# Attention masks as bfloat16 products, maxima of four heads at once, and a second batch's sums moved

## The chip, the cores and the metric

The kernel runs on one core of a Trainium2 chip. The metric is the device time of one execution in microseconds (us). A core has five engines, each of which works through its own list of instructions in order and waits for the others by semaphores: TensorE (PE, with its weight loads PEld), VectorE (DVE), ScalarE (ACT), GpSimd (POOL) and SyncE (SP), which here issues all the DMAs.

## The reference

Two batches of 8 heads, 768 positions, head dimension 64, all in float32. Each query sees the keys less than 16 positions away and, beside them, 24 block summaries of its batch: per block of 32 positions the maximum of the keys and the mean of the values. The result goes through two feed-forward networks (512 to 2048 to 512), one after the other.

```python
k_sum = k.reshape(B, H, nb, 32, D).max(axis=3)
v_sum = v.reshape(B, H, nb, 32, D).mean(axis=3)
scores_l = np.where(abs(pos[:, None] - pos[None, :]) < 16, scale * q @ k.T, -1e9)
scores_s = scale * np.einsum('bhsd,bhnd->bhsn', q, k_sum) + np.log(32)
a = softmax(np.concatenate([scores_l, scores_s], axis=-1))
x = np.matmul(a, np.concatenate([v, v_sum], axis=2))
g = h - np.tanh(h)                # first network,  h = x @ w_in;  x = g @ w_out
g = h * np.tanh(softplus(h))      # second network, the same way
```

## The kernel before

The attention works in 12 units of 128 queries (units 0 to 5 are batch 0, units 6 to 11 batch 1). A unit has two row halves of 64 queries (`s`) and two head parities (`e`); with four pairs of heads (`hp`) that gives, for each `e`, a PSUM bank of 4 x 120 scores: 24 summaries and 96 window keys. The banks of `e` = 0 have the tag `s`, those of `e` = 1 the tag `tr`, two buffers each; `v_trans` takes a `tr` bank as well.

Everything is issued by one hand-written loop over steps j = 0 to 31. Each engine gets its instructions in that order. For unit u:

- step 2u: `qk(u)`, the products of queries and keys on TensorE (line 310). It needs `k_fill(u)`, which copies the block maxima into both ends of the unit's key tile (line 263).
- steps 2u+1 and 2u+2: `softmax(u, 0)` and `softmax(u, 1)`. On VectorE one instruction for each pair of heads adds the mask and reduces to the negated maximum (line 324); on ScalarE one exponential for each follows, with its sum (line 329).
- step 2u+3: `norm(u)`, reciprocals on VectorE (lines 336, 339), then one product for each `e` (line 341), on GpSimd, or on VectorE where `NORM_DVE` says so.
- steps 2u+5 and 2u+6: `a_trans(u, e)`, four transposes on TensorE (line 349) and a copy out of PSUM (lines 353 on VectorE, 355 on ScalarE, by `ASB_DVE`).
- step 2u+7: `av(u)`, the products with the values (line 363); steps 2u+8 and 2u+9: `x_hi` and `x_lo` split the result in two parts (lines 371, 375).

Within a step the order is `x_hi`, `qk`, `softmax`, weight conversions (`AHEAD`), `norm`, `x_lo`, `a_trans`, `av`, then a list `todo` filled by `at(step, ...)`: loads, `k_sum` (block maxima, line 255), `k_fill`, `v_sum` (block sums, line 272 on VectorE or lines 276 and 280 on GpSimd), and last more conversions (`AFTER`). A conversion (`conv_tick`) splits a piece of the weights, over ScalarE (`conv_top`, line 114; `conv_hi`), VectorE (`conv_or`, line 121; `conv_lo`, line 137) and, in the steps of `HI_POOL` and `LO_POOL`, GpSimd.

At steps 24, 25 and 29 the loop issues the first products of the first network (`more_in`), whose first 512 tokens are units 0 to 3. After the loop come 96 network steps.

Of the kernel before, what the change touches and what calls it, by code (L numbers as in the profile page):

```python
# [2 lines left out]

# [6 lines left out]
F32 = mybir.dt.float32  # L10
# [16 lines left out]
def kernel(  # L27
# [32 lines left out]
    BIG = 1.0e30  # L60
# [5 lines left out]
    n_raw, n_cv = 6, 5  # L66
# [11 lines left out]
    def pst(tag):  # L78
        return ps.tile([128, 512], F32, tag=tag, name=tag)
# [88 lines left out]

    ASB_DVE = (0, 2, 7, 11, 12, 13, 14, 15, 17, 20, 21)
    NORM_DVE = (0, 13, 21, 23)
    FILL_DVE = (0, 1, 4, 5, 6, 7, 8, 9, 11)
    AHEAD = {23: 1, 24: 3, 29: 3, 31: 1}
    AFTER = {19: 1, 21: 1, 22: 1, 25: 1, 28: 3, 30: 1}
    HI_POOL = (19, 21, 22, 24, 25, 30)
# [2 lines left out]
    def attention(actx):  # L179
        con = actx.enter_context(tc.tile_pool(name="con", bufs=1, side="right"))  # L180
        two = actx.enter_context(tc.tile_pool(name="two", bufs=2, side="right"))
# [3 lines left out]
        NK = UPB + 2  # L185
        kt = [kq.tile([128, HP, KU + 2 * NB], F32, name=f"kt{n}") for n in range(NK)]
        qt = [kq.tile([128, HP, 128], F32, name=f"qt{n}") for n in range(3)]
        vu = [con.tile([KA, 2, H, D], F32, name=f"vu{n}") for n in range(3)]
        masks = [con.tile([128, KA], F32, name=f"mask{m}") for m in range(3)]
        ident = con.tile([128, 128], F32, name="ident")  # L190
        SUM = ((0, NB), (KW, KA))
        WND = ((NB, KA), (0, KW))

        def constants():
            nonlocal tops
            make_identity(nc, ident)
            k_edges(0)
            for m in range(3):
                nc.gpsimd.memset(masks[m], 0.0)
                for s in range(2):  # L200
                    rows = masks[m][T * s:T * s + T]
                    nc.gpsimd.memset(rows[:, SUM[s][0]:SUM[s][1]], math.sqrt(D) * math.log(BLK))
                    reg = rows[:, WND[s][0]:WND[s][1]]

                    conds = [([[1, KW]], -1, -1), ([[-1, KW]], 2 * WIN - 1, 1)]
                    if (m, s) == (0, 0):
                        conds.append(([[1, KW]], -WIN, 0))
                    if (m, s) == (2, 1):
                        conds.append(([[-1, KW]], KW - WIN - 1, 0))
                    for pattern, base, mul in conds:  # L210
                        nc.gpsimd.affine_select(
                            out=reg, in_=reg, pattern=pattern, base=base, channel_multiplier=mul,
                            compare_op=ALU.is_ge, fill=-BIG,
                        )
            k_edges(UPB)
            tops = top_tiles(2)

        vtc, ksum, vsum = {}, {}, {}
# [39 lines left out]
            )  # L258

        def k_fill(u):  # L260
            eng = nc.vector if u in FILL_DVE else nc.gpsimd
            for o in (0, NB + KU):
                eng.tensor_copy(kt[u % NK][:, :, o:o + NB], ksum[u // UPB])

        def v_sum(b, g, part, pool=False):
            if b not in vsum:
# [31 lines left out]
        sums, neg, aa, asb, xps, sc = {}, {}, {}, {}, {}, {}  # L298

        def qk(u):  # L300


            for e in range(2):
                sc[u, e] = pst(("s", "tr")[e])[:, 0:HP * KA].rearrange("p (a n) -> p a n", a=HP)
            for hp in range(HP):
                for s in range(2):
                    for e in range(2):
                        d = slice(64 * e, 64 * e + 64)
                        k0 = s * (NB + T)
                        nc.tensor.matmul(  # L310
                            out=sc[u, e][T * s:T * s + T, hp, :],
                            lhsT=qt[u % 3][d, hp, T * s:T * s + T],
                            rhs=kt[u % NK][d, hp, k0:k0 + KA],
                        )

        def softmax(u, e):
            w, pv = u % UPB, sc.pop((u, e))
            if e == 0:
                aa[u] = two.tile([128, 2, HP, KA], F32, tag="aa", name="aa", bufs=3)
                neg[u] = two.tile([128, 2, HP], F32, tag="neg", name="neg", bufs=3)  # L320
                sums[u] = two.tile([128, 2, HP], F32, tag="sums", name="sums", bufs=3)
            m = masks[0 if w == 0 else 2 if w == UPB - 1 else 1]
            for hp in range(HP):
                nc.vector.tensor_tensor_reduce(  # L324
                    out=aa[u][:, e, hp, :], in0=pv[:, hp, :], in1=m, scale=-1.0 / math.sqrt(D),
                    scalar=3.0e38, op0=ALU.add, op1=ALU.min, accum_out=neg[u][:, e, hp:hp + 1],
                )
            for hp in range(HP):
                nc.scalar.activation(  # L329
                    out=aa[u][:, e, hp, :], in_=aa[u][:, e, hp, :], func=ACTF.Exp,  # L330
                    scale=-1.0, bias=neg[u][:, e, hp:hp + 1], accum_out=sums[u][:, e, hp:hp + 1],
                )

        def norm(u):
            r = two.tile([128, 2, 2, HP], F32, tag="rd", name="rd")
            nc.vector.tensor_scalar(
                out=r[:, 0], in0=sums[u], scalar1=1.0e-9, scalar2=None, op0=ALU.add
            )
            nc.vector.reciprocal(out=r[:, 1], in_=r[:, 0])
            for e in range(2):  # L340
                (nc.vector if 2 * u + e in NORM_DVE else nc.gpsimd).tensor_tensor(
                    out=aa[u][:, e], in0=aa[u][:, e],
                    in1=r[:, 1, e, :].unsqueeze(2).to_broadcast([128, HP, KA]), op=ALU.mult,
                )

        def a_trans(u, e):
            p = pst("aT")
            for hp in range(HP):
                nc.tensor.transpose(p[0:KA, hp * 128:(hp + 1) * 128], aa[u][:, e, hp, :], ident)
            t = two.tile([KA, HP, 128], F32, tag=f"asb{e}", name="asb")  # L350
            pv = p[0:KA, :].rearrange("p (a n) -> p a n", a=HP)
            if 2 * u + e in ASB_DVE:
                nc.vector.tensor_copy(t, pv)
            else:
                nc.scalar.activation(out=t, in_=pv, func=ACTF.Copy)
            asb[u, e] = t
# [26 lines left out]
        def at(u, *fs):  # L383
            todo.setdefault(u, []).extend(fs)
# [28 lines left out]
        at(4, L(load_k, 8), L(v_sum, 0, 1, 0), L(v_sum, 0, 2, 0), L(v_sum, 0, 2, 1, True))  # L413
        before_av[5] = L(v_trans, 0)
        at(5, L(v_fill, 1), L(v_fill, 2), L(load_k, 9), L(load_k, 10))
        at(5, L(k_sum, 6))
        at(6, L(k_sum, 7))
        at(7, L(k_sum, 8), L(load_k, 11))
        at(8, L(k_sum, 9), L(load_vt, 1, 0))
        at(9, L(k_sum, 10), L(load_vt, 1, 1))  # L420
        at(10, L(k_sum, 11), L(k_fill, 6))
        at(11, L(load_vt, 1, 2), L(v_sum, 1, 0, 0))
        at(12, L(v_sum, 1, 0, 1, True), L(conv_ahead, n_raw))
        at(13, L(v_sum, 1, 1, 0))
        at(14, L(v_sum, 1, 1, 1, True))
        at(15, L(v_sum, 1, 2, 0, True))
        at(16, L(v_sum, 1, 2, 1))
        before_av[17] = L(v_trans, 1)
        at(17, L(v_fill, 1), L(v_fill, 2))
        for u in range(7, 12):  # L430
            at(2 * u - 3, L(k_fill, u))
        NJ = 2 * NU
        LT, LA = 5, 6

# [4 lines left out]
        for j in range(NJ + LA + 2):  # L439
            if j in (NJ, NJ + 1, NJ + 5):  # L440
                more_in(n_in)
            if j == NJ:
                kq_x.close()
                more_w(4)
            xu, xr = divmod(j - LA - 2, 2)
            if xu >= 0 and not xr:
                x_hi(xu)
            if j < NJ and j % 2 == 0:
                qk(j // 2)
            nu, nr = divmod(j - 3, 2)  # L450
            nr = nr == 0 and 0 <= nu < NU
            if 1 <= j <= NJ:
                softmax(*divmod(j - 1, 2))
            ticks(j, AHEAD)
            if nr:
                norm(nu)
            if xu >= 0 and xr:
                x_lo(xu)
            if LT <= j < NJ + LT:
                a_trans(*divmod(j - LT, 2))  # L460
            if j in before_av:
                before_av[j]()
# [295 lines left out]
```

## Time and profile before

| | us |
|---|---|
| median of 3 runs (range) | 602.61 (602.38 to 603.33) |
| profiled execution: its time | 603.07 |
| its span, first to last instruction | 601.3 |
| busy in the span: PE, DVE, ACT, POOL | 578.8, 417.8, 328.5, 53.4 |

The span is 1.77 us shorter than the execution's time. In the slices of the page, of 15 us each, TensorE is at nine tenths or more from the ninth on; POOL works in the first six and hardly after. Matmul times overlap one another, so a busy TensorE in the attention isn't an engine at its limit.

### The profile page before, as it was taken

How to read it: one execution, taken by the hardware profiler on the slowest of the kernel's cores; microseconds unless marked ns; L12 is line 12 of the kernel's file. 1: busy time of each engine (PE TensorE's matmuls, PEld its weight loads, DVE VectorE, ACT ScalarE, POOL GpSimd, SP SyncE). 2: the span in 40 equal slices, each digit the busy share in tenths (PEclk: the TensorE clock that was granted, in tenths of full speed). 3: DMA queues.
4: the chain of work that ended last, by engine and by line, in shares of the span. 5: the costliest groups of instructions: out<-in, count | busy, mean ns of one | idle time of the engine just before them, and what ended most of it. 6: DMA issues, size and time to landing. Idle time of an engine off the chain costs nothing.

```text
span 601.3 us, 9203 instructions
## 1 busy us (share of the span) xinstructions
PE 578.8 (96%) x3212; PEld 479.0 (80%) x3212; DVE 417.8 (69%) x968; ACT 328.5 (55%) x791; POOL 53.4 (9%) x109
## 2 busy tenths in 40 slices
PE   6768899999999999999999999999999999999997
PEld 5556788888888888888888888888888888888885
DVE  5797978886251222377776489997688777597785
ACT  4788878885251122367765456664464444454442
POOL 6465660000000000000000000000000000000000
PEclk9798899999999999999999999999999999999999
DMA  9997567765020000226661102100100000100001
GB/s 271 257 306 213 154 184 238 222 218 168 0 88 0 1 0 1 62 88 192 197 186 43 40 8 63 52 2 1 55 16 1 1 1 0 71 1 1 1 1 70
DMA packets 32110, 52.20 MB, mean 87 GB/s; under 512 B 3200, under 2 KB 25728, under 8 KB 32064
## 3 DMA queue, kind: packets, MB, share of 16 engines
q1 hardware_dynamic: 32064, 51.62, 28.5%
q8 instruction: 25, 0.41, 0.3%
q14 instruction: 21, 0.17, 0.1%
HBM read 48.07 MB, written 3.15 MB: 85 GB/s over the span
## 4 chain that ended last, share of the span: by engine, by line
PE 88%; DMA 4%; DVE 3%; ACT 2%; SPq 1%; issue 1%; POOL 0%; ACTq 0%
PE aT L478 7%; PE aT L479 7%; PE tr L479 7%; PE x L479 7%; PE aT L480 7%; PE tr L480 7%; PE x L480 7%; PE x L478 7%; PE tr L478 7%; PE s L479 7%; PE s L478 7%; PE s L480 7%; DMA kt<-in_kw_dram 3%; ACT aa L329 1%; DMA vtc<-in_vt_dram 1%; PE x L363 1%
## 5 line engine op out<-in xcount | busy, mean ns | idle before, releaser
L503 DVE TENSOR_TENSOR glo<-t,ghi 128x512 fp32r<-128x512 f32 x48 | 33.4, 695 | 85.4 <-ACT ghi L498 85.4
L498 ACT ACTIVATE ghi<-t 128x512 fp32r<-128x512 f32 x48 | 30.2, 629 | 96.5 <-PE tr L480 96.5
L478 PE MATMUL aT<-xhi,w 128*128 128x512 f32 x192 | 74.9, 390 | 0.0
L478 PE MATMUL s<-xhi,w 128*128 128x512 f32 x192 | 74.9, 390 | 0.0
L480 PE MATMUL s<-xhi,w 128*128 128x512 f32 x192 | 74.7, 389 | 0.0
L480 PE MATMUL aT<-xhi,w 128*128 128x512 f32 x192 | 74.7, 389 | 0.0
L479 PE MATMUL s<-xlo,w 128*128 128x512 f32 x192 | 74.7, 389 | 0.0
L479 PE MATMUL aT<-xlo,w 128*128 128x512 f32 x192 | 74.7, 389 | 0.0
L114 ACT ACTIVATE top<-raw 128x256 f16<-128x256 bf16 x128 | 61.5, 486 | 12.2 <-ACT w L132 4.8
L121 DVE SCALAR_TENSOR_TENSOR cv<-raw,top 128x256 int32<-128x256 int32 x128 | 55.4, 434 | 11.8 <-ACT top L114 7.6
L132 ACT ACTIVATE w<-cv 128x256 fp32r<-128x256 f32 x120 | 47.6, 402 | 10.7 <-DVE cv L121 9.8
L137 DVE TENSOR_TENSOR w<-cv,w 128x256 fp32r<-128x256 f32 x114 | 48.4, 426 | 0.1
L534 DVE SCALAR_TENSOR_TENSOR t<-n,r 128x512 f32<-128x512 f32 x48 | 33.1, 689 | 17.4 <-ACT r L531 17.3
L503 DVE TENSOR_TENSOR glo<-n,ghi 128x512 fp32r<-128x512 f32 x48 | 33.1, 690 | 15.5 <-ACT ghi L498 15.5
L498 ACT ACTIVATE ghi<-n 128x512 fp32r<-128x512 f32 x48 | 30.3, 632 | 24.4 <-PE tr L479 16.1
L329 ACT ACTIVATE aa<-aa,neg 128x120 f32<-128x120 f32 x96 | 36.6, 384 | 12.4 <-DVE neg L324 12.4
L480 PEld LDWEIGHTS aT<-xhi,w 128*128 128x128 f32 x192 | 36.1, 188 | 7.5
L480 PEld LDWEIGHTS s<-xhi,w 128*128 128x128 f32 x192 | 36.1, 188 | 7.5
L478 PEld LDWEIGHTS aT<-xhi,w 128*128 128x128 f32 x192 | 36.0, 188 | 7.5
L478 PEld LDWEIGHTS s<-xhi,w 128*128 128x128 f32 x192 | 36.0, 188 | 7.5
L479 PEld LDWEIGHTS s<-xlo,w 128*128 128x128 f32 x192 | 36.0, 188 | 7.4
L479 PEld LDWEIGHTS aT<-xlo,w 128*128 128x128 f32 x192 | 36.0, 188 | 7.4
(97 smaller groups left out, 1293.1 us busy)
## 6 DMA issues: line engine op xcount, KB each, us to landing
raw<-in_w_dram SPq DMA_DIRECT2D x128, 255.8 KB, 3.6
vu<-in_vw_dram SPq DMA_DIRECT2D x24, 192.0 KB, 4.9
qt<-in_qt_dram SPq DMA_DIRECT2D x12, 256.0 KB, 4.9
vtc<-in_vt_dram SPq DMA_DIRECT2D x6, 512.0 KB, 6.7
out_dram<-o SPq DMA_DIRECT2D x9, 256.0 KB, 2.0
kt<-in_kw_dram SPq DMA_DIRECT2D x6, 320.0 KB, 8.5
kt<-in_kw_dram SPq DMA_DIRECT2D x6, 256.0 KB
out_dram<-t SPq DMA_DIRECT2D x3, 256.0 KB
```

Of the source, the lines that this page charges most:

```text
L114: nc.scalar.activation(out=tops[n % len(tops)].bitcast(F16).rearrange("p (n t) -> p n t", t=2)[:, :, 1], in_=raws[n].bitcast(BF16).rearran ...
L121: nc.vector.scalar_tensor_tensor(out=tmps[n], in0=raws.pop(n).bitcast(I32).rearrange("p (n t) -> p n t", t=2)[:, :, 0], scalar=13, in1=top ...
L132: nc.scalar.activation(out=hi, in_=t, func=ACTF.Copy)
L137: (nc.gpsimd if on_pool else nc.vector).tensor_tensor(out=W[i][:, 1, o:o + PW], in0=tmps.pop(n).bitcast(F32), in1=W[i][:, 0, o:o + PW].bit ...
L329: nc.scalar.activation(out=aa[u][:, e, hp, :], in_=aa[u][:, e, hp, :], func=ACTF.Exp, scale=-1.0, bias=neg[u][:, e, hp:hp + 1], accum_out= ...
L363: nc.tensor.matmul(out=xps[u][64 * e:64 * e + 64, hp, T * s:T * s + T], lhsT=vu[u % 3][:, s, 2 * hp + e, :], rhs=asb[u, e][:, hp, T * s:T ...
L478: nc.tensor.matmul(out=out, lhsT=w[0], rhs=x[0], start=first, stop=False)
L479: nc.tensor.matmul(out=out, lhsT=w[0], rhs=x[1], start=False, stop=False)
L480: nc.tensor.matmul(out=out, lhsT=w[1], rhs=x[0], start=False, stop=last)
L498: nc.scalar.activation(out=ghi, in_=t, func=ACTF.Copy)
L503: nc.vector.tensor_tensor(out=glo, in0=t, in1=ghi.bitcast(F32), op=ALU.subtract)
L534: nc.vector.scalar_tensor_tensor(out=ts[z], in0=ns[z], scalar=2.0, in1=rs[z], op0=ALU.add, op1=ALU.mult)
```

## The change

Each unit's mask becomes part of the products. Four matmuls in bfloat16 (for each `e` and `s` one of 128 rows, 64 columns, 4 x 120 outputs) write the mask to PSUM first, and the score products accumulate on it. There are four masks, by half and by whether the unit is at the batch's edge. VectorE then takes one maximum over a whole bank for each `e` and scales both at once (`max_`, at the odd step, for both `e`); the exponentials read PSUM instead of SBUF. `k_fill` is one instruction, on GpSimd for all units but 0 and 1; all products of `norm` are GpSimd's; the copies of `e` = 1 are all VectorE's and those of `e` = 0 all ScalarE's. For batch 1, `k_sum` moves from steps 5 to 10 to steps 8 to 11, `k_fill(6)` from step 10 to step 11, the later fills by one step, the last load of values from step 11 to 10, and all of `v_sum` is VectorE's, in steps 12 to 16.

```diff
-            for m in range(3):
-                nc.gpsimd.memset(masks[m], 0.0)
...
+            nc.gpsimd.tensor_copy(sel[0:T], ident[0:T, 0:T])
+            nc.gpsimd.memset(sel[T:128], 1.0)
+            for (s, edge), m in masks.items():
+                nc.gpsimd.memset(m, 0.0)
+                left = float(np.float32(math.sqrt(D) * math.log(BLK)))
+                for r in range(3):
...
+                    nc.gpsimd.affine_select(
+                        out=reg, in_=reg, pattern=[[0, NB]], base=-(T + r), channel_multiplier=1,
+                        compare_op=ALU.not_equal, fill=part,
+                    )
...
         def k_fill(u):
-            eng = nc.vector if u in FILL_DVE else nc.gpsimd
-            for o in (0, NB + KU):
-                eng.tensor_copy(kt[u % NK][:, :, o:o + NB], ksum[u // UPB])
+            t = kt[u % NK]
+            o = bass.AP(t.tensor, t.offset, [t.ap[0], [NB + KU, 2], [KU + 2 * NB, HP], [1, NB]])
+            (nc.vector if u < 2 else nc.gpsimd).tensor_copy(
+                o, ksum[u // UPB].unsqueeze(1).to_broadcast([128, 2, HP, NB])
+            )
...
         def qk(u):
+            w = u % UPB
             for e in range(2):
                 sc[u, e] = pst(("s", "tr")[e])[:, 0:HP * KA].rearrange("p (a n) -> p a n", a=HP)
+            for e in range(2):
+                for s in range(2):
+                    m = masks[s, int(w == (0, UPB - 1)[s])]
+                    nc.tensor.matmul(
+                        out=sc[u, e][T * s:T * s + T], lhsT=sel,
+                        rhs=m.unsqueeze(1).to_broadcast([128, HP, KA]), start=True, stop=False,
+                    )
...
-                            rhs=kt[u % NK][d, hp, k0:k0 + KA],
+                            rhs=kt[u % NK][d, hp, k0:k0 + KA], start=False, stop=hp == HP - 1,
...
+        def max_(u):
+            m = two.tile([128, 2, HP], F32, tag="max", name="max")
+            neg[u] = two.tile([128, 2, HP], F32, tag="neg", name="neg")
+            for e in range(2):
+                nc.vector.tensor_reduce(out=m[:, e], in_=sc[u, e], axis=AX.X, op=ALU.max)
+            nc.vector.tensor_scalar(
+                out=neg[u], in0=m, scalar1=-1.0 / math.sqrt(D), scalar2=None, op0=ALU.mult
+            )
...
-            for hp in range(HP):
-                nc.vector.tensor_tensor_reduce(
-                    out=aa[u][:, e, hp, :], in0=pv[:, hp, :], in1=m, scale=-1.0 / math.sqrt(D),
-                    scalar=3.0e38, op0=ALU.add, op1=ALU.min, accum_out=neg[u][:, e, hp:hp + 1],
-                )
             for hp in range(HP):
                 nc.scalar.activation(
-                    out=aa[u][:, e, hp, :], in_=aa[u][:, e, hp, :], func=ACTF.Exp,
-                    scale=-1.0, bias=neg[u][:, e, hp:hp + 1], accum_out=sums[u][:, e, hp:hp + 1],
+                    out=aa[u][:, e, hp, :], in_=pv[:, hp, :], func=ACTF.Exp,
+                    scale=1.0 / math.sqrt(D), bias=neg[u][:, e, hp:hp + 1],
+                    accum_out=sums[u][:, e, hp:hp + 1],
                 )
...
-                (nc.vector if 2 * u + e in NORM_DVE else nc.gpsimd).tensor_tensor(
+                nc.gpsimd.tensor_tensor(
...
-            if 2 * u + e in ASB_DVE:
+            if e:
...
-        at(5, L(k_sum, 6))
-        at(6, L(k_sum, 7))
-        at(7, L(k_sum, 8), L(load_k, 11))
-        at(8, L(k_sum, 9), L(load_vt, 1, 0))
-        at(9, L(k_sum, 10), L(load_vt, 1, 1))
-        at(10, L(k_sum, 11), L(k_fill, 6))
-        at(11, L(load_vt, 1, 2), L(v_sum, 1, 0, 0))
-        at(12, L(v_sum, 1, 0, 1, True), L(conv_ahead, n_raw))
-        at(13, L(v_sum, 1, 1, 0))
-        at(14, L(v_sum, 1, 1, 1, True))
-        at(15, L(v_sum, 1, 2, 0, True))
+        at(7, L(load_k, 11))
+        at(8, L(load_vt, 1, 0), L(k_sum, 6), L(k_sum, 7))
+        at(9, L(load_vt, 1, 1), L(k_sum, 8), L(k_sum, 9))
+        at(10, L(load_vt, 1, 2), L(k_sum, 10))
+        at(11, L(k_sum, 11), L(k_fill, 6))
+        at(12, L(conv_ahead, n_raw), L(v_sum, 1, 0, 0))
+        at(13, L(v_sum, 1, 0, 1), L(v_sum, 1, 1, 0))
+        at(14, L(v_sum, 1, 1, 1))
+        at(15, L(v_sum, 1, 2, 0))
...
-            at(2 * u - 3, L(k_fill, u))
+            at(2 * u - 2, L(k_fill, u))
...
+            if j < NJ and j % 2 == 1:
+                max_(j // 2)
             if 1 <= j <= NJ:
-                softmax(*divmod(j - 1, 2))
+                exps(*divmod(j - 1, 2))
```

## Rows read from the trace of the kernel before

**Rows 1.** Stretches: busy PE, PEld, DVE, ACT, POOL (instructions), clock, DMA share, GB/s.
```profile
80.00:100.00 20.00, 20.00 (x116) 16.38 (x115) 15.01 (x34) 16.30 (x43) 6.21 (x8) 1.00 0.73 219
```
**Rows 2.** TensorE in order of time: start, us, instruction, count [idle <-releaser].
```profile
62.11 1.15 PE L363 MATMUL x<-asb,vu 120*64 120x64 f32 x30 [1.65 <-DVE asb L353]
63.18 0.40 PE L310 MATMUL s<-kt,qt 64*64 64x120 f32 x1
...
76.76 0.62 PE L349 MATMUL aT<-ident,aa 128*120 128x128 f32 x4 [0.16 <-POOL aa L341]
```
**Rows 3.** Groups by line and shape, 0 to 90 us: busy, mean ns | idle.
```profile
L329 ACT ACTIVATE aa<-aa,neg 128x120 f32<-128x120 f32 x96 | 36.6, 384 | 12.4 <-DVE neg L324 12.4
...
L255 DVE TENSOR_REDUCE ksum<-kt 128x16 f32<-128x512 f32 x12 | 8.2, 685 | 10.3 <-DMA kt<-in_kw_dram 10.1
...
L353 DVE COPY asb<-aT 120x512 f32<-120x512 f32 x11 | 7.4, 674 | 2.9 <-PE aT L349 2.9
L371 ACT ACTIVATE xhi<-x 128x512 fp32r<-128x512 f32 x12 | 7.0, 583 | 1.6 <-PE x L363 1.6
...
L263 DVE COPY kt<-ksum 128x96 f32<-128x96 f32 x18 | 5.8, 377 | 0.1
...
L211 POOL TENSOR_SCALAR_AFFINE_SELECT mask<-mask 64x96 f32<-64x96 f32 x14 | 3.7, 261 | 0.8
...
L341 DVE TENSOR_TENSOR aa<-aa,rd 128x480 f32<-128x480 f32 x4 | 3.0, 753 | 0.1
...
L263 POOL COPY kt<-ksum 128x96 f32<-128x96 f32 x6 | 1.4, 265 | 0.0
```
**Rows 4.** VectorE in order of time, 10 to 48 us.
```profile
35.54 0.28 DVE L324 CUSTOM_DVE_ANT_0 aa<-s,mask 128x120 f32<-128x120 f32 x1
...
35.74 0.28 DVE L324 CUSTOM_DVE_ANT_0 aa<-s,mask 128x120 f32<-128x120 f32 x1
...
36.35 0.17 DVE L336 TENSOR_SCALAR rd<-sums 128x8 f32<-128x8 f32 x1
...
36.67 0.64 DVE L375 TENSOR_TENSOR xlo<-x,xhi 128x512 fp32r<-128x512 f32 x1
37.23 0.68 DVE L272 TENSOR_REDUCE vsum<-vtc 128x16 f32<-128x512 f32 x1
```
**Rows 5.** The page's costliest groups: busy, mean ns | idle before.
```profile
L498 ACT ACTIVATE ghi<-t 128x512 fp32r<-128x512 f32 x48 | 30.2, 629 | 96.5 <-PE tr L480 96.5
```
**Rows 6.** Chain that ended last: start, us, what.
```profile
30.19 4.37 DMA kt<-in_kw_dram
...
79.56 0.23 PE aT L479
```
**Rows 7.** TensorE in order of time, 27 to 55 us.
```profile
27.68 0.31 PE L310 MATMUL s<-kt,qt 64*64 64x120 f32 x1
...
36.13 0.31 PE L310 MATMUL s<-kt,qt 64*64 64x120 f32 x1
...
37.11 0.65 PE L349 MATMUL aT<-ident,aa 128*120 128x128 f32 x4
...
46.03 1.84 PE L363 MATMUL x<-asb,vu 120*64 120x64 f32 x30 [2.22 <-ACT asb L355]
...
54.65 0.31 PE L310 MATMUL tr<-kt,qt 64*64 64x120 f32 x1 [1.18 <-ACT vu L287]
```
**Rows 8.** GpSimd in order of time.
```profile
11.13 1.97 POOL L276 TENSOR_TENSOR vtc<-vtc 128x256 f32<-128x256 f32 x4 [2.94 <-DMA vtc<-in_vt_dram]
...
36.92 1.94 POOL L341 TENSOR_TENSOR aa<-aa,rd 128x480 f32<-128x480 f32 x2 [3.61 <-DVE rd L339]
```
**Rows 9.** ScalarE in order of time.
```profile
40.69 0.38 ACT L329 ACTIVATE aa<-aa,neg 128x120 f32<-128x120 f32 x1
...
53.41 1.18 ACT L287 ACTIVATE vu<-tr 24x512 f32<-24x512 f32 x2
```
**Rows 10.** A stretch of 5 us, columns as in the first group.
```profile
45.00:50.00 5.00, 3.97 (x66) 3.55 (x66) 3.71 (x18) 5.00 (x23) 3.92 (x9) 0.66 1.07 299
```

More of the change, by code (lines that the diff above doesn't have):

```diff
@@ L2 @@
 import math
+import numpy as np
 import concourse.bass as bass
@@ L167, in conv_tick @@
             n2 += 1
-    ASB_DVE = (0, 2, 7, 11, 12, 13, 14, 15, 17, 20, 21)
-    NORM_DVE = (0, 13, 21, 23)
-    FILL_DVE = (0, 1, 4, 5, 6, 7, 8, 9, 11)
     AHEAD = {23: 1, 24: 3, 29: 3, 31: 1}
@@ L188, in attention @@
         vu = [con.tile([KA, 2, H, D], F32, name=f"vu{n}") for n in range(3)]
-        masks = [con.tile([128, KA], F32, name=f"mask{m}") for m in range(3)]
+        masks = {z: con.tile([128, KA], BF16, name=f"mask{z[0]}{z[1]}") for z in ((0, 0), (0, 1), (1, 0), (1, 1))}
+        sel = con.tile([128, T], BF16, name="sel")
         ident = con.tile([128, 128], F32, name="ident")
@@ L197, in constants @@
             k_edges(0)
-            for m in range(3):
-                nc.gpsimd.memset(masks[m], 0.0)
[L200 to L213, printed above, removed]
-                        )
+            nc.gpsimd.tensor_copy(sel[0:T], ident[0:T, 0:T])
[4 more added lines that the diff above has]
+                for r in range(3):
+                    part = float(np.float32(left).astype(mybir.dt.np(BF16)))
+                    left -= part
+                    reg = m[:, SUM[s][0]:SUM[s][1]]
+                    nc.gpsimd.affine_select(
+                        out=reg, in_=reg, pattern=[[0, NB]], base=-(T + r), channel_multiplier=1,
+                        compare_op=ALU.not_equal, fill=part,
+                    )
+                assert left == 0.0
+                reg = m[0:T, WND[s][0]:WND[s][1]]
+                conds = [([[1, KW]], -1, -1), ([[-1, KW]], 2 * WIN - 1, 1)]
+                if edge:
+                    conds.append((([[1, KW]], -WIN, 0), ([[-1, KW]], KW - WIN - 1, 0))[s])
+                for pattern, base, mul in conds:
+                    nc.gpsimd.affine_select(
+                        out=reg, in_=reg, pattern=pattern, base=base, channel_multiplier=mul,
+                        compare_op=ALU.is_ge, fill=-BIG,
+                    )
             k_edges(UPB)
@@ L312, in qk, with exps @@
                             lhsT=qt[u % 3][d, hp, T * s:T * s + T],
-                            rhs=kt[u % NK][d, hp, k0:k0 + KA],
+                            rhs=kt[u % NK][d, hp, k0:k0 + KA], start=False, stop=hp == HP - 1,
                         )
-        def softmax(u, e):
-            w, pv = u % UPB, sc.pop((u, e))
+        def max_(u):
[5 more added lines that the diff above has]
+                out=neg[u], in0=m, scalar1=-1.0 / math.sqrt(D), scalar2=None, op0=ALU.mult
+            )
+        def exps(u, e):
+            pv = sc.pop((u, e))
             if e == 0:
                 aa[u] = two.tile([128, 2, HP, KA], F32, tag="aa", name="aa", bufs=3)
-                neg[u] = two.tile([128, 2, HP], F32, tag="neg", name="neg", bufs=3)
                 sums[u] = two.tile([128, 2, HP], F32, tag="sums", name="sums", bufs=3)
-            m = masks[0 if w == 0 else 2 if w == UPB - 1 else 1]
-            for hp in range(HP):
-                nc.vector.tensor_tensor_reduce(
-                    out=aa[u][:, e, hp, :], in0=pv[:, hp, :], in1=m, scale=-1.0 / math.sqrt(D),
-                    scalar=3.0e38, op0=ALU.add, op1=ALU.min, accum_out=neg[u][:, e, hp:hp + 1],
-                )
             for hp in range(HP):
                 nc.scalar.activation(
-                    out=aa[u][:, e, hp, :], in_=aa[u][:, e, hp, :], func=ACTF.Exp,
-                    scale=-1.0, bias=neg[u][:, e, hp:hp + 1], accum_out=sums[u][:, e, hp:hp + 1],
+                    out=aa[u][:, e, hp, :], in_=pv[:, hp, :], func=ACTF.Exp,
+                    scale=1.0 / math.sqrt(D), bias=neg[u][:, e, hp:hp + 1],
+                    accum_out=sums[u][:, e, hp:hp + 1],
                 )
```

## The prediction

> **What bounds the kernel now.** I read the stretches first, then TensorE in order of time at the end of the attention, then the groups by line, and last each engine's timeline through the attention. In the stretches TensorE is busy 20.00 of 20 us from 80 us on, at full clock [rows 1]: the networks run at TensorE's pace, and no edit touches them. In its timeline the last real wait is the one of 1.65 us before `av(7)` at 62.11; the products of the last unit, `qk(11)`, follow at 63.18, and up to the end the reader finds only 0.16 us more, before the transposes of unit 11 at 76.76, which wait for GpSimd's `norm` [rows 2]. So the change is worth what it shifts two points, `qk(11)` at 63.18 and those transposes at 76.76. All that lies behind them, some 525 us, stays.
>
> What paces the units is seen in the groups: ScalarE's exponentials wait 12.4 us for VectorE's maxima, and VectorE's block maxima 10.1 us for DMAs of keys [rows 3]. VectorE is the bound, with DMA behind it at the start.
>
> **The change part by part.** *Prices.* Before, the masked maxima of a bank are four instructions that start 0.20 us apart [rows 4], 1.6 us a unit, and the first exponential can go after one of them. Now both banks come first. The nearest row is the reduction of 512 elements, 685 ns [rows 3]; on 480 about 0.64, of which some 0.08 overlaps the next (the row of 0.64 us at 36.67 is followed at 37.23 [rows 4]): 0.56 each, and with the scaling, like the small row of 0.17, 1.4 us until the first exponential. Bounds: 1.2 (pure proportion to an instruction without fixed part) and 1.6 (two full 685 and the small one). [...]
>
> An exponential takes 384 ns from SBUF [rows 3]. ScalarE's 512-element operation takes 583 ns from PSUM [rows 3] and 629 from SBUF [rows 5], so I take 46 ns off each: 1.35 us for the four of a bank, at worst the old 1.54.
>
> A mask product has 480 columns. The 512-column product is spaced 0.23 us [rows 6], so four cost 0.9 us one after the other and 0.45 if the two row halves overlap as `qk`'s do (all of `qk` takes 0.98 from 36.13 to 37.11 [rows 7]). I take 0.4 where nothing hides them, 0.2 where the first bank's run ahead during a wait; bounds 0 (all ahead) and 0.9, twice that at half clock. The transposes cost 0.65 less an overlap, 0.5.
>
> GpSimd's normalization takes 1.94 for two [rows 8]. Its fill of twice the elements I put at 0.45, between one old instruction and two (0.265 and 0.53) [rows 3]. The new masks need 22 selections for 14; eight more at 0.26 are 2.1 us [rows 3], and GpSimd stands 2.94 us before its next work at 11.13, waiting for values [rows 8]. That cover hides them; without it, batch 0's sums come up to 2 us later.
>
> *What it takes off VectorE.* Eighteen fills cost it 5.8 us and four normalizations 3.0 [rows 3]; the maxima fall by 0.2 a unit, 2.4. Three block sums come back, 3 x 0.6. Net some 9 us of busy time, and the waits for keys move to where their data have landed: the last keys of unit 11 land at 30.19 + 4.37 = 34.56 [rows 6]. This is the gain of the change, if VectorE's busy time sets the pace.
>
> *What it puts in order on the path.* I follow unit 4 to unit 6 through the new order. `qk(4)` starts behind `av(0)`, as before at 27.7 [rows 7]: what came earlier there (no wait for the keys of unit 6) is given back to the later maxima of unit 2 and 3. With masks 27.7 + 0.4 + 0.9 = 29.0, transposes 29.5. From here VectorE has no gap: copy 0.6, `k_sum` 6 and 7 1.2, `max_(4)` 1.4, reciprocals and `x_lo` 0.32 + 0.56 [rows 4], `k_sum` 8 and 9 1.2, copy 0.6, `k_sum(10)` 0.6, `max_(5)` 1.4, reciprocals 0.3: 8.2 us, to 37.7. Only then can GpSimd normalize unit 4, 1.9 us, and only behind that stands `k_fill(6)`, 0.45, which VectorE did before; `qk(6)` needs it. It starts at 40.0 instead of 36.13 [rows 7]. This is the new wait: queued behind `qk(6)` on TensorE are the transposes and `av` of unit 3, and behind these the copies. First exponential of unit 6: 40.0 + 0.9 + 0.5 + copy 0.6 + block sum 0.6 + 1.4 = 44.0, before 40.69 [rows 9]: 3.3 late.
>
> *What it gains then.* A bank is now held until its exponentials are done, so two units make a loop: second masks 0.2, `qk` 0.9, transposes 0.5, copy 0.6, block sum 0.6, `max_` 1.4, exponentials 1.35, copy and `x_hi` on ScalarE 1.0, exponentials 1.35: 7.9 us, 3.95 a unit. Before, units 6 to 11 took (63.18 - 36.13) / 5 = 5.4 [rows 2, 7]. So `qk(8)` at 47.9. `qk(9)` waits, as before, for the evacuation of the block means (1.18 us; the wait before 54.65 is it [rows 7, 9]), which stands behind the exponentials of unit 8: 0.9 + 0.5 + 0.6 + 0.9 (rest of a sum, a sum) + 1.4 + 1.35 + 0.5 + 1.2 + 0.2 = 7.55, at 55.4. Two units more without sums, with the weight conversions of steps 19 and 21 (some 0.9 on ScalarE and VectorE): 8.2, `qk(11)` at 63.6, before 63.18: +0.4.
>
> *The end.* From `qk(11)` to its transposes TensorE has 13.6 us of other work and waits 0.16 for GpSimd [rows 2]. Now the maxima come 1.2 later than the first of them did (1.4 for 0.2), two rounds of exponentials give 0.4 back, and GpSimd has a second product of unit 10 to do, 1.0, half of it in its waits for conversions: the transposes slip by another 0.8, +1.2 in all.
>
> [...]
>
> Sum: +0.4 + 0.8 + 0.9 = +2.1 on the profiled 603.07; its median lies 0.46 lower, 602.61 + 2.1 = 604.7. What can be told from no change is about 0.2%, 1.2 us. The likeliest case's own range is 603.6 to 607.
>
> **Rivals.** *VectorE's relief wins (faster).* If the path to `k_fill(6)` is shorter than I think, because unit 3 runs at full clock (1.4 earlier) and the masks are free (0.4 and 0.2 each time), `qk(6)` starts at 38 and everything behind moves by 2, the clock stays up (0.9 back) and a unit costs 0.2 less: 604.7 - 2 - 0.9 - 1 = 600.8, down to 599 if `max_` takes 1.2. It decides where `qk(6)` starts: before 38.5 the five units behind make it up. For it: 9 us less on the engine for which 12.4 us are waited. Against: `k_fill(6)` stands in an order list, and no free time of VectorE shortens it.
>
> *It comes out even.* `qk(6)` at 39, no loss to the clock: 603. For it: the loop is 1.4 a unit faster over five units, so each delay ahead of it is paid back in part.
>
> [...]
>
> **How the numbers follow.** Forecast and slower still together 0.57 (0.42 and 0.15), even 0.2, faster by VectorE's relief 0.23. Slower by more than 0.2%: 0.57; within: 0.2; faster: 0.23. The range reaches from the relief's middle, 599.8, to the third rival's 607.8: it leaves out a tenth at each end.
>
> **What would show it.** `max_` at 1.2 to 1.6 us a unit; exponentials at 0.34; `qk(6)` waiting for GpSimd's fill until about 40; then units 4 us apart, with a gap before `qk(9)`; clock below 1.00 behind these two gaps; TensorE without waits from about 64. The forecast is wrong if `qk(6)` starts by 38, or if `qk(11)` starts before 62.

## The result, and the profile after

The kernel after took 608.92 us (median, 607.65 to 609.65), beside 602.50 for the kernel before on the same chip: 1.0107 times before, 95% interval 1.0079 to 1.0136. In a later round it took 608.42 beside 604.07, 1.0073 times (1.0053 to 1.0093). So the change costs 4.4 to 6.4 us. The prediction said slower, 604.7, and its range ended at 607.8. The span of the profiled execution is 607.8 us, before it was 601.3.

First the stretches of the kernel after (columns as in [rows 10]).

```profile
20.00:25.00 5.00, 2.35 (x10) 0.63 (x8) 1.63 (x6) 3.46 (x14) 3.27 (x7) 0.50 1.11 295
25.00:30.00 5.00, 5.00 (x78) 4.32 (x76) 1.92 (x5) 1.01 (x6) 0.00 (x0) 0.67 0.48 128
40.00:45.00 5.00, 2.50 (x35) 2.19 (x36) 1.21 (x3) 3.69 (x18) 2.51 (x4) 0.70 1.04 312
```

The new trouble lies at two places, and one of them is early: from 20 to 30 us VectorE works 3.55 of 10 us, and the granted clock is 0.50 and then 0.67. Then the groups by line, 0 to 95 us (busy, mean ns | idle before), which answer to [rows 3]:

```profile
L363 POOL TENSOR_TENSOR aa<-aa,rd 128x480 f32<-128x480 f32 x24 | 23.6, 1003 | 32.3 <-DVE rd L361 32.3
...
L350 ACT ACTIVATE aa<-s,neg 128x120 f32<-128x120 f32 x48 | 16.7, 359 | 22.0 <-DVE rd L358 14.8 <-DVE neg L340 4.7 <-DVE rd L361 2.5
...
L339 DVE TENSOR_REDUCE max<-s 128x4 f32<-128x480 f32 x12 | 7.8, 650 | 2.4 <-PE tr L329 2.4
...
L320 PE MATMUL tr<-mask,sel 128*64 128x480 bf16 x24 | 5.7, 424 | 3.5 <-ACT vu L298 3.0 <-ACT aa L350 0.5
...
L272 POOL COPY kt<-ksum 128x192 f32<-128x192 f32 x10 | 3.2, 348 | 0.0
```

The prices came out near what was taken: a maximum of four heads 650 ns, an exponential from PSUM 359 (0.34 us from start to start), the double fill 348. ScalarE's exponentials waited 12.4 us for VectorE before [rows 3] and wait 22.0 now, though VectorE has less to do. The row of the masks holds the clue: 3.0 us of waiting for ScalarE's `vu` (L298), the evacuation of the value means.

TensorE in order of time: first two lines of the kernel before that [rows 2, 7] don't have, then the kernel after.

```profile
21.94 0.31 PE L310 MATMUL tr<-kt,qt 64*64 64x120 f32 x1 [1.12 <-ACT vu L287]
...
78.67 0.65 PE L349 MATMUL aT<-ident,aa 128*120 128x128 f32 x4
```

```profile
21.71 0.60 PE L296 MATMUL tr<-ident,vsum 128*24 128x128 f32 x2 [0.95 <-POOL vsum L291]
22.24 0.61 PE L320 MATMUL s<-mask,sel 128*64 128x480 bf16 x2
24.55 0.61 PE L320 MATMUL tr<-mask,sel 128*64 128x480 bf16 x2 [1.70 <-ACT vu L298]
25.09 0.46 PE L329 MATMUL s<-kt,qt 64*64 64x120 f32 x1
...
26.90 1.76 PE L371 MATMUL aT<-ident,aa 128*120 128x128 f32 x8
...
30.28 0.31 PE L329 MATMUL tr<-kt,qt 64*64 64x120 f32 x1
...
42.51 0.46 PE L329 MATMUL s<-kt,qt 64*64 64x120 f32 x1 [2.96 <-POOL kt L272]
...
52.52 0.31 PE L329 MATMUL s<-kt,qt 64*64 64x120 f32 x1
...
69.45 0.31 PE L329 MATMUL s<-kt,qt 64*64 64x120 f32 x1
...
85.12 0.65 PE L371 MATMUL aT<-ident,aa 128*120 128x128 f32 x4
```

`qk(3)` starts at 25.09 (`L329` is `qk`, `L320` its masks), `qk(4)` at 30.28, `qk(6)` at 42.51 behind GpSimd's fill, `qk(8)` at 52.52, `qk(11)` at 69.45, the last transposes of unit 11 at 85.12 (before 78.67). `qk(11)` is 6.3 us later than before, so the loss has arisen by then, and 2.6 us of it by `qk(4)`, where the prediction had only the 0.4 of the masks. ScalarE and VectorE at that place:

```profile
21.48 0.36 ACT L350 ACTIVATE aa<-s,neg 128x120 f32<-128x120 f32 x1 [2.15 <-DVE rd L358]
...
22.84 0.61 ACT L377 ACTIVATE asb<-aT 120x512 f32<-120x512 f32 x1
23.32 1.18 ACT L298 ACTIVATE vu<-tr 24x512 f32<-24x512 f32 x2
24.53 0.36 ACT L350 ACTIVATE aa<-tr,neg 128x120 f32<-128x120 f32 x1
```

```profile
21.50 0.20 DVE L361 RECIPROCAL rd<-rd 128x8 f32<-128x8 f32 x1
28.05 0.69 DVE L375 COPY asb<-aT 120x512 f32<-120x512 f32 x1 [6.35 <-PE aT L371]
28.66 0.65 DVE L339 TENSOR_REDUCE max<-s 128x4 f32<-128x480 f32 x1
```

Read them together. The second masks of `qk(3)` go at 24.55, when the evacuation (23.32 to 24.5) is done: they need the bank of `v_trans`. Unit 2's own `tr` bank is not to be had, since its exponentials read it only from 24.53 on. The kernel before waited for the same evacuation, 1.12 us up to 21.94; now it comes later: on ScalarE it stands behind the first exponentials of unit 2 (from 21.48, before from 19.18), and these wait for both maxima. On TensorE the transposes of the unit before stand behind `qk(3)` (26.90); VectorE waits 6.35 us for these at its copy, and the maxima of unit 3, queued behind the copy, begin at 28.66.

### The profile page after: what moved, and what is told of

The parts are those of the page before. It is cut to its first block, busy times and chain, and to the rows that moved or that the text cites. A ratio compares the mean times of both kernels' runs of the same rounds, so it can differ in the third digit from the quotient of the medians.

```text
span 607.8 us, 9137 instructions
## 1 busy us (share of the span) xinstructions
PE 583.3 (96%) x3260; PEld 478.1 (79%) x3260; DVE 409.7 (67%) x796; ACT 325.0 (53%) x790; POOL 52.6 (9%) x107
## 4 chain that ended last, share of the span: by engine, by line
PE 88%; DVE 5%; DMA 2%; ACT 2%; issue 1%; POOL 1%; SPq 1%; ACTq 0%; POOLq 0%
PE aT L500 7%; PE aT L501 7%; PE tr L501 7%; PE x L501 7%; PE aT L502 7%; PE tr L502 7%; PE x L502 7%; PE x L500 7%; PE tr L500 7%; PE s L501 7%; PE s L502 7%; PE s L500 7%; DVE max L339 2%; DMA vtc<-in_vt_dram 2%; ACT aa L350 1%; PE s L329 1%
## 5 line engine op out<-in xcount | busy, mean ns | idle before, releaser
L116 ACT ACTIVATE top<-raw 128x256 f16<-128x256 bf16 x128 | 61.8, 489 | 12.4 <-issue 4.5
L541 ACT ACTIVATE t<-aT 128x512 f32<-128x512 f32 x24 | 14.4, 599 | 44.7 <-PE aT L502 29.1
```

What stands on the lines that cost most here:

```text
L116: nc.scalar.activation(out=tops[n % len(tops)].bitcast(F16).rearrange("p (n t) -> p n t", t=2)[:, :, 1], in_=raws[n].bitcast(BF16).rearran ...
L541: nc.scalar.activation(out=t, in_=hs[z], func=ACTF.Exp)
```

## The experiments

Each kernel was compared with the kernel before on its own chip; the numbers are ratios with 95% intervals. Runs told under one heading shared a chip.

**The two parts apart.** First the order alone: the kernel before with the moved sums, the fills (one instruction, a step later) and normalizations on GpSimd and the copies by parity, but its masked maxima as they were. Then the masks alone: masks, maxima and exponentials of after, with the order and the engine lists of before.

```diff
# order alone, against before
-        at(5, L(k_sum, 6))
-        at(6, L(k_sum, 7))
...
+        at(8, L(load_vt, 1, 0), L(k_sum, 6), L(k_sum, 7))
+        at(9, L(load_vt, 1, 1), L(k_sum, 8), L(k_sum, 9))
...
# masks alone, against after: the same lines the other way round, and
+                (nc.vector if 2 * u + e in NORM_DVE else nc.gpsimd).tensor_tensor(
+            if 2 * u + e in ASB_DVE:
```

> The kernel before with the new order and the new engines alone (moved block maxima and sums, fills and normalizations on GpSimd, copies by parity); masks and maxima stay as before. Theory P (the loss is a longer path through each unit: mask products, whole-bank maxima ahead of the first exponential, banks held by the exponentials, and on top the wait of the products of unit 6 for GpSimd's fill): only the last of these is here, and VectorE has less to do; 0 to +3 us against before, products of unit 6 at 37.5 to 39 us. Rival O (the order and the engines are what costs): +5 to +7 us.

> The changed kernel with the order and the engines of before: mask products, whole-bank maxima and exponentials from PSUM alone. Theory P: +3 to +5 us against before, with the products of units 1 to 4 already 1 to 3 us late. Rival O: -1 to +1 us. If P and O each hold a part, this and the order alone add up to the +6.4 us of the whole change.

Measured: order alone 0.9985 (0.9966 to 1.0004), no change that can be told; masks alone 1.0036 (1.0021 to 1.0052), +2.2 us. The theory that the order is the cost falls, and the masks alone cost less than the 3 to 5 us of the other theory. But -0.9 and +2.2 don't make the +4.4 to +6.4 of both: the parts act on each other. Where, is read from TensorE, with the order alone and then with the masks alone:

```profile
19.85 0.39 PE L284 MATMUL tr<-ident,vsum 128*24 128x128 f32 x2 [0.96 <-POOL vsum L279]
20.18 0.31 PE L309 MATMUL s<-kt,qt 64*64 64x120 f32 x1
...
24.43 0.31 PE L309 MATMUL s<-kt,qt 64*64 64x120 f32 x1 [0.70 <-DMA qt<-in_qt_dram]
```

```profile
22.54 0.61 PE L321 MATMUL tr<-mask,sel 128*64 128x480 bf16 x2 [1.97 <-ACT vu L299]
...
28.97 0.31 PE L330 MATMUL s<-kt,qt 64*64 64x120 f32 x1
```

With the order alone `qk(3)` follows the value transposes at once, at 20.18, 0.1 us before the evacuation even begins (20.28): the masked maxima have carried unit 2's scores to SBUF by 19.9. `qk(4)` starts at 24.43, 3.3 us earlier than before. With the masks alone `qk(3)` waits for the evacuation too (1.97 us), and `qk(4)` starts at 28.97, 1.3 later than before. Added up, the two would make it some 2.0 earlier; it is 2.6 later.

**The fill of unit 6 on VectorE, and the clock kept up.** Both on the kernel after, on the same chip as the two above. The extra mask products are overwritten by the real ones; no work is left out.

```diff
-            (nc.vector if u < 2 else nc.gpsimd).tensor_copy(
+            (nc.vector if u in (0, 1, 6) else nc.gpsimd).tensor_copy(
# the other kernel, in qk
+            for _ in range({3: 4, 6: 10, 9: 6}.get(u, 0)):
+                for s in range(2):
+                    nc.tensor.matmul(
+                        out=sc[u, 0][T * s:T * s + T], lhsT=sel,
+                        rhs=masks[s, 0].unsqueeze(1).to_broadcast([128, HP, KA]), start=True, stop=True,
+                    )
```

> The changed kernel with one instruction moved: the fill of unit 6 on VectorE instead of GpSimd, so that it no longer stands behind the normalization of unit 4. Theory P: the products of unit 6 start 1.5 to 2 us earlier (near 40.7 instead of 42.5) and the time falls by as much, to +4.4 to +5 us against before. A rival in which unit 6 only catches up on something else late (keys, banks): no change, +6 to +6.5 us.

> The changed kernel with extra mask products (overwritten by the real ones) ahead of units 3, 6 and 9, where TensorE waits, so that it stays busy there; the result is the same. [...] Theory P: the products and transposes behind unit 6 run at full clock, -1 to -1.5 us, +5 to +5.5 against before. If the extra products only delay the real ones, no gain: +6.4 or more.

Measured: fill 1.0068 (1.0049 to 1.0087), clock 1.0051 (1.0032 to 1.0069). Against the kernel after as first measured both look like a gain, and the clock's +3.1 us lies below the +5 to +5.5 expected of full clock behind unit 6 alone. Against its second measurement, 1.0073 (1.0053 to 1.0093), neither is told apart from no gain. The trace of the fill agrees: from `qk(4)` to `qk(6)` it took 12.06 us, with the fill on GpSimd 12.23. With the extra products the granted clock from 25 to 30 us was 1.00 instead of 0.67, and from 40 to 45 it was 1.00 instead of 0.70. `qk(3)` still started late, at 23.68, but `qk(4)` followed at 27.57, where it was in the kernel before:

```profile
23.68 0.31 PE L335 MATMUL s<-kt,qt 64*64 64x120 f32 x1
...
27.57 0.31 PE L335 MATMUL s<-kt,qt 64*64 64x120 f32 x1
```

So what the wait before `qk(3)` costs is in part, by this comparison, the half clock of the work behind it: 0.50 from 25 to 28 us in the kernel after.

**A bank for the values.** The value transposes take a bank of the tag of `av`. One edit; then the same in the kernel before; then with the fill on VectorE.

```diff
         def v_trans(b):
-            p = pst("tr")
+            p = pst("x")
```

> The kernel after, with one edit: the transposes of the block sums of values take a PSUM bank of the tag of av (x) in place of one of the scores' second tag (tr). Theory B (banks): since the exponentials read the scores in PSUM, unit 2's bank is held until E(2,1) is done, so qk(3) takes the bank of the value transposes and waits for their evacuation, which ScalarE does behind E(2,0) (wait to 24.55 in the kernel after, 1.70 us); the same before qk(9) (wait to 60.09, 1.29 us). With a bank of its own, qk(3) starts some 2.5 us earlier (22.5 instead of 25.1), qk(9) some 1.5 us earlier on top, and 3 to 4 us of this reach the end: 1.001 to 1.0035 times before, against the 1.0107 of the kernel after. Theory P (only the terms of the prediction: maxima, block sums, fill, masks): the wait only shows where ScalarE is late, the same lateness comes out in the maxima right behind: within 1 us of the kernel after, 1.009 or more.

> The kernel before with the same edit alone (value transposes in a bank of av's tag). Theory B: before, the masked maxima carry the scores to SBUF and free the bank early, and VectorE sets the pace; its waits for the evacuation (1.12 us before 21.94, and the one before 54.65) are mostly made up: -1.5 to 0 us, 0.9975 to 1.0. If the bank is worth as much here (3 us or more), the bank is a fault of both kernels and no reason for the difference between them.

> The kernel after with the bank of e5 and the fill of unit 6 on VectorE (as in the run with that fill alone, which took 2.3 us off). Theory B with P: the two lie at different places (before qk(3) and qk(9); before qk(6)) and add: 5 to 6 us off, 0.998 to 1.002 times before. Theory P without B: as the fill alone, 1.006 to 1.008.

Measured: the kernel after with the bank 1.0014 (0.9990 to 1.0038); the kernel before with the bank 0.9997 (0.9976 to 1.0018); bank and fill 1.0011 (0.9988 to 1.0034). The bank takes nearly the whole loss off the kernel after and does nothing for the kernel before, as the theory of the banks said. With the fill too the time lies in the range expected of both, but the fill adds nothing to the bank that can be told (1.0011 against 1.0014). One pair of lines of the kernel with both, GpSimd and then VectorE, shows why it is no bargain:

```profile
36.42 1.93 POOL L363 TENSOR_TENSOR aa<-aa,rd 128x480 f32<-128x480 f32 x2 [2.66 <-DVE rd L361]
```

```profile
37.44 1.03 DVE L272 COPY kt<-ksum 128x192 f32<-128x192 f32 x1
```

Beside GpSimd's normalization the fill takes VectorE 1.03 us, three times GpSimd's 0.35, and ends at 38.47; GpSimd is through with the normalization at 38.35.

**What is left: clock and maxima.** On the kernel with bank and fill: ten pairs of extra products ahead of unit 6; the maxima scaled bank by bank, so that the first exponentials need one reduction; both.

```diff
             for e in range(2):
                 nc.vector.tensor_reduce(out=m[:, e], in_=sc[u, e], axis=AX.X, op=ALU.max)
-            nc.vector.tensor_scalar(
-                out=neg[u], in0=m, scalar1=-1.0 / math.sqrt(D), scalar2=None, op0=ALU.mult
-            )
+                nc.vector.tensor_scalar(
+                    out=neg[u][:, e], in0=m[:, e], scalar1=-1.0 / math.sqrt(D), scalar2=None, op0=ALU.mult
+                )
```

> The kernel of the run with the bank and the fill of unit 6 on VectorE (1.0011 times before), with ten pairs of extra mask products ahead of unit 6, whose result the real masks overwrite: no work is left out, TensorE only stays busy during its wait of 2.79 us before qk(6). Theory C (clock): there the granted clock of the stretch behind that wait was 0.83, and the transposes of unit 4 and av(4) took 1.72 and 1.33 us against 1.09 and 1.15 at full clock; with the clock kept 1.0 in that stretch, qk(6) as before and qk(7) up to 1.0 earlier, -0.5 to -1.5 us at the end: 0.9985 to 1.0003. Rival (slack): the lateness behind qk(6) falls where VectorE sets the pace: no change, 1.0011 with +-0.001.

> The kernel with the bank and the fill on VectorE, and the scaling of the maxima made bank by bank (reduce, scale, reduce, scale), so that the exponentials of the first bank can start after one reduction. Theory T (the prediction's term: 1.4 us of maxima stand ahead of every first exponential): the first exponential of a unit comes 0.6 us earlier, in some six units this is on the path, -2 to -4 us: 0.9945 to 0.998. Rival V: VectorE is full in these stretches (4.93 of 5 us), and one instruction more a unit (0.1 us) takes back what the earlier exponentials give: 1.0011 with +-0.0012.

> Both edits together. If C and T both hold: -2.5 to -5.5 us from 1.0011, 0.992 to 0.997, faster than both kernels. If neither: 1.0011.

Measured: clock 1.0019 (1.0003 to 1.0035), split 1.0047 (1.0029 to 1.0065), both 1.0041 (1.0022 to 1.0059). Neither gains, and the split is slower than both of its theories said. It did what it was made for, as its VectorE and ScalarE show at unit 4:

```profile
30.63 0.65 DVE L339 TENSOR_REDUCE max<-s 128x4 f32<-128x480 f32 x1
31.31 0.17 DVE L340 TENSOR_SCALAR neg<-max 128x4 f32<-128x4 f32 x1
31.39 0.65 DVE L339 TENSOR_REDUCE max<-tr 128x4 f32<-128x480 f32 x1
...
32.16 0.17 DVE L358 TENSOR_SCALAR rd<-sums 128x8 f32<-128x8 f32 x1
```

```profile
31.60 0.36 ACT L350 ACTIVATE aa<-s,neg 128x120 f32<-128x120 f32 x1 [1.27 <-DVE neg L340]
```

The first exponential comes 0.97 us after the first reduction starts; unsplit, in the kernel with bank and fill, it was 1.53 (29.93 to 31.46). So the 1.4 us of `max_` ahead of the exponentials is real, but taking 0.56 of it away per unit gave nothing. On VectorE the split makes `max_` 0.20 us longer (30.63 to 32.16, unsplit 29.93 to 31.26), twice what was expected, and VectorE is busy 4.90 of 5 us from 30 to 35 in this kernel, 4.93 without the split. A full VectorE that loses 0.20 us a unit fits the loss, but no run shows that it is the reason.

**The masks alone with the bank; the order alone with fill and clock.** The first is the kernel of the masks alone with the line of `v_trans` above, the second the kernel of the order alone with the fill on VectorE and products of the identity ahead of units 2 and 6 (overwritten too).

```diff
+            for _ in range({2: 6, 6: 10}.get(u, 0)):
+                nc.tensor.matmul(out=sc[u, 0][:, 0, :], lhsT=ident, rhs=ident[:, 0:KA], start=True, stop=True)
```

> The kernel of the masks alone (the order and the engines of before; 1.0036 times before), with the value transposes in a bank of av's tag. Theory B: what the masks cost by themselves is the held bank (qk(3) at 23.07 behind ScalarE's evacuation, before 21.94): it falls to 0.998 to 1.0015. Rival (masks, maxima and the block sums ahead of them on VectorE are the cost): 1.003 to 1.0045, as without the bank.

> The kernel of the order alone (masked maxima as before; 0.9985 times before), with the fill of unit 6 on VectorE and extra products of the identity, overwritten, ahead of unit 2 (6) and of unit 6 (10), so that TensorE is busy in its waits of 1.31 and 2.14 us there (the granted clock behind them was 0.59 and 0.50); no work is left out. Theory C: the half clock behind these waits takes some 2 us, of which half reaches the end, and the fill 0.5 to 1: 0.9955 to 0.998, faster than before. Rival: VectorE sets the pace (4.97 of 5 us busy from 30 and from 45), the two are slack: 0.998 to 1.0.

Measured: 1.0024 (1.0004 to 1.0044) and 0.9985 (0.9965 to 1.0004). The first lies between its two theories and settles nothing. The second is where the order alone was, as its rival said: no version was found that beats the kernel before for certain.

**Which of the two waits.** The kernel after unchanged, with the bank for batch 0 alone, and for batch 1 alone, on one chip.

```diff
-            p = pst("tr")
+            p = pst("tr" if b else "x")
# the other kernel
+            p = pst("x" if b else "tr")
```

> The kernel after, unchanged, on the chip of the next two. If the chips don't differ in what the change costs, 1.008 to 1.0135 times before. If it comes out at 1.007 or less, the runs with the fill and with the clock kept lie within what chips differ, and only the bank's edit is shown.

> The kernel after with only batch 0's value transposes in a bank of av's tag (the wait before qk(3), for which the prediction had no term). Theory B0: most of the bank's worth lies here, because the lateness of qk(3) is followed by half clock: 3 to 4.5 us less than the kernel after beside it, 1.003 to 1.006. Theory B9 (the wait before qk(9) carries it): 1 to 1.5 us less.

> The kernel after with only batch 1's value transposes in a bank of av's tag (the wait of 1.29 us before qk(9), which the prediction had in its loop). Theory B0: 1 to 1.5 us less than the kernel after beside it. Theory B9: 3 us less or more.

Measured: unchanged 1.0073 (1.0053 to 1.0093), batch 0's bank 1.0020 (1.0001 to 1.0038), batch 1's 1.0067 (1.0046 to 1.0088). The wait before `qk(3)` carries the loss, 3.2 us of 4.4. The bank for batch 1 gives nothing that can be told, but this doesn't say what the wait before `qk(9)` is worth: there `av(5)`, whose tag the value transposes then use, waits 1.82 us instead, and from `qk(8)` to `qk(9)` it took 8.2 us, in the kernel unchanged 8.1. TensorE with batch 0's bank:

```profile
20.63 0.39 PE L296 MATMUL x<-ident,vsum 128*24 128x128 f32 x2 [1.30 <-POOL vsum L291]
20.95 0.39 PE L320 MATMUL s<-mask,sel 128*64 128x480 bf16 x2
21.18 0.37 PE L320 MATMUL tr<-mask,sel 128*64 128x480 bf16 x2
21.48 0.31 PE L329 MATMUL s<-kt,qt 64*64 64x120 f32 x1
...
22.46 1.09 PE L371 MATMUL aT<-ident,aa 128*120 128x128 f32 x8
...
25.83 0.31 PE L329 MATMUL s<-kt,qt 64*64 64x120 f32 x1 [0.38 <-DMA qt<-in_qt_dram]
...
38.06 0.31 PE L329 MATMUL s<-kt,qt 64*64 64x120 f32 x1 [2.96 <-POOL kt L272]
...
46.79 0.31 PE L329 MATMUL s<-kt,qt 64*64 64x120 f32 x1
...
63.71 0.31 PE L329 MATMUL s<-kt,qt 64*64 64x120 f32 x1
...
79.38 0.65 PE L371 MATMUL aT<-ident,aa 128*120 128x128 f32 x4
```

Its VectorE:

```profile
23.15 0.69 DVE L375 COPY asb<-aT 120x512 f32<-120x512 f32 x1 [2.83 <-PE aT L371]
23.76 0.65 DVE L339 TENSOR_REDUCE max<-s 128x4 f32<-128x480 f32 x1
```

TensorE and VectorE with batch 1's bank, where the wait before `qk(3)` stands as in the kernel after:

```profile
23.21 0.61 PE L320 MATMUL tr<-mask,sel 128*64 128x480 bf16 x2 [1.50 <-ACT vu L298]
23.75 0.46 PE L329 MATMUL s<-kt,qt 64*64 64x120 f32 x1
25.56 1.96 PE L371 MATMUL aT<-ident,aa 128*120 128x128 f32 x8
...
29.53 0.31 PE L329 MATMUL s<-kt,qt 64*64 64x120 f32 x1
...
56.64 1.98 PE L385 MATMUL x<-asb,vu 120*64 120x64 f32 x32 [1.82 <-issue]
```

```profile
26.70 0.69 DVE L375 COPY asb<-aT 120x512 f32<-120x512 f32 x1 [6.35 <-PE aT L371]
27.31 0.65 DVE L339 TENSOR_REDUCE max<-s 128x4 f32<-128x480 f32 x1
```

These two are the pair to compare: in both the last values of batch 0 were there at 18.0 us, and the evacuation began at 21.94 and 21.98. (In the profile of the kernel after they came at 19.3, in its second profile at 18.7: this differs between executions of the same early work, so up to 1.3 us of that profile's lateness at `qk(3)` is not the bank's.) With batch 0's bank the masks of `qk(3)` follow the value transposes without a gap, and its products start at 21.48 instead of 23.75. The transposes behind take 1.09 us, at a granted clock of 1.00 (20 to 25 us), instead of 1.96; VectorE waits 2.83 us instead of 6.35; the maxima of unit 3 start 3.6 us earlier and `qk(4)` 3.7. Some 2 of these 3.7 us are, by an estimate, the lower clock behind the wait: with the extra products, at 1.00 from 25 to 30 us, `qk(4)` started 3.89 us after `qk(3)` (23.68 to 27.57), with batch 1's bank 5.78 (23.75 to 29.53). The bank takes away both, and the runs don't divide the 3.2 us between them.

With batch 0's bank `qk(4)` starts at 25.83, 1.85 us earlier than before. `qk(11)` is at 63.71, the last transposes of unit 11 at 79.38, before at 78.67: +0.7.

## Why the prediction was wrong

The step that failed is the start of the path: "`qk(4)` starts behind `av(0)`, as before at 27.7 [rows 7]: what came earlier there (no wait for the keys of unit 6) is given back to the later maxima of unit 2 and 3." It set the gain of the order against the price of the maxima and left the wait of `qk(3)` for a bank as it was. With 0.4 for the masks it puts the products of `qk(4)` at 28.1; they started at 30.28 (30.14 and 29.53 in two other profiles with that wait). The prediction knew both halves of the mechanism: it wrote that a bank is now held until its exponentials are done, and it put the evacuation of the block means into the loop of `qk(9)`. It didn't ask the same of the first evacuation, before `qk(3)`, nor for the half clock behind it (0.50 from 25 to 28 us).

With that wait taken away by a bank, the time is 1.0020 times before, +1.2 us (interval +0.1 to +2.3), which holds the forecast of +2.1, and `qk(11)` is at 63.71, by the sum 63.6. That agreement is luck. `qk(4)` then starts at 25.83, 2.3 us before the 28.1 of the sum: of the 3.3 us that the order alone gives there 1.85 is left, where the sum gave all of it back. And the pieces behind it are longer than the sum had them: 12.2 us for 11.9 up to `qk(6)`, 8.7 for 7.9 up to `qk(8)`, 16.9 for 15.75 up to `qk(11)`, together 2.3.

Point by point, first the kernel after as profiled:

- *Prices*: right. Reductions 650 ns and 0.56 apart, exponentials 0.34 apart (1.35 for four), normalization 1.93 for two, fill 0.35 against the 0.45 taken; a unit's masks, 0.53 at a granted clock of 1.00 (20.95 to 21.48 above), cost a little more than the 0.4 taken. The first exponential of a unit starts 1.53 after the first reduction, 0.13 more than the 1.4 taken. For the reduction, 685 ns for 512 elements from SBUF [rows 3] makes 642 for 480 in proportion, and 650 were measured from PSUM.
- *VectorE's relief*: some 8 us instead of 9. The fills of units 0 and 1 stay on VectorE (0.4 us), and it has twelve copies of 0.69 now instead of eleven.
- *`qk(4)` to `qk(6)`*: right. 11.9 us by the sum (28.1 to 40.0), 12.2 measured. `qk(6)` waits for GpSimd's fill behind the normalization, as said, at 42.51 only because `qk(4)` was late. That the fill's place is what costs there was wrong: on VectorE it came 0.2 sooner. What is left for the cost is VectorE's work ahead of it; no run took that away.
- *The two-unit loop behind `qk(6)`*: mis-sized. 7.9 us by the sum, 10.0 measured (42.5 to 52.5), of which 1.3 goes, by an estimate, with the lower clock (0.70 from 40 to 45 us; 8.7 from 38.06 to 46.79 with batch 0's bank, where the clock is 1.00 throughout).
- *`qk(8)` to `qk(11)`*: mis-sized. 15.75 by the sum, 16.9 measured; each unit was taken some 0.4 too short.
- *The end*: +0.8 by the sum, though its items as they stand make 1.3 (1.2 - 0.4 + 0.5); +0.2 measured: 15.7 us from `qk(11)` to the last transposes of unit 11, before 15.5 (63.18 [rows 2] to 78.67).
- *The clock*: +0.9 by the sum for `qk(6)` and `qk(9)`. That was the author's estimate, and no run shows it as a term by itself. What the runs showed is where the clock fell: in the kernel after as profiled it fell at `qk(6)` (0.70 from 40 to 45 us) but not at `qk(9)` (1.00 from 55 to 65; 0.66 from 55 to 60 in the second profile of this kernel), and it was low from 10 to 30 us (0.63, 0.50, 0.50 and 0.67 in stretches of 5 us), where the sum had no term. Keeping it up ahead of `qk(6)` (1.00 from 35 to 45 us, without the extra products 0.82 and 0.83) took off nothing that can be told once the bank was right (1.0019 against 1.0011).

By `qk(11)` the steps miss 2.2 (`qk(4)`), 0.3, 2.1, 0.4 and 0.8, together 5.8; of this 0.8 had been charged to the end and 0.9 to the clock, and 4.1 remains, nearly all of the way from +2.1 to the +6.3 at which `qk(11)` stands.

Of the rivals, that of VectorE's relief named the sign that decides, `qk(6)` before 38.5, and the sign failed: with batch 0's bank `qk(6)` starts at 38.06, and the kernel then is even or slightly slower, not faster, for the loop behind it is slower than that rival took. The third rival, slower still, came nearest in time: the range ends at its 607.8. But exponentials at the old 0.38 us [rows 9] didn't come, they are 0.34 apart; masks at half clock did, at `qk(3)` (0.61 us for a pair at 0.50). What stays open is why the last 1 us or so remains: neither the fill's place, nor the clock, nor the 0.56 us of the second reduction gave it back.

## What to carry to other kernels

When an instruction that copied data out of a PSUM bank is dropped and its successor reads the bank itself, the bank is held by another engine and for longer: list every user of that bank's tag, the rare ones too, and find for each whose work stands ahead of it in the new holder's queue. Here one stray user cost 3.2 us, in part, by an estimate, by the half clock (0.50) behind its wait, and a changed tag took it away. And test the parts of a change apart before explaining their sum: -0.9 and +2.2 made +4.4 or more, and the rest came only with both. When two profiles are compared, look first whether their inputs landed at the same time: here up to 1.3 us of a difference came from that.

## What the runs showed of the hardware

- The fill of 128 x 192, 0.35 us on GpSimd, took VectorE 1.03 us while GpSimd normalized beside it, and ended 0.12 us after GpSimd's product; with GpSimd idle, at 10.03 in the kernel after, it took VectorE 0.26. In the kernel before, VectorE's two half fills took 1.11 us from 37.82 on, beside GpSimd's product [rows 8], and 0.33 us at 35.30, with GpSimd idle.
- Two mask products on separate halves of the rows took 0.37 and 0.39 us as a pair at a granted clock of 1.00 (at 20.95 and 21.18 with batch 0's bank), 0.61 at 0.50 (at 22.24 and 24.55 in the kernel after); the four of a unit put 0.53 us ahead of `qk` at 1.00 (20.95 to 21.48).
- The granted clock from 10 to 15 and from 15 to 20 us differed between two executions of the kernel after itself (0.63 and 0.50; 0.72 and 0.59) and among its near kin with the same early work: 1.00 and 0.66 with batch 0's bank, 1.00 and 1.00 with the bank for both. `qk(11)` of the two executions lies 0.4 us apart (69.45 and 69.02). So the verdicts here rest on the medians, not on single profiles.
